# Key projection by token tiles, a norm transposed by TensorE, early FFN gradient tiles and a last store in halves, in a backward-and-forward transformer block

## The chip, the cores and the metric

The kernel runs on one core of a Trainium2 chip. The metric is device time in microseconds (us) of one execution, as the median of several runs. TensorE (PE) multiplies matrices, VectorE (DVE) and ScalarE (ACT) work on elements, GpSimd (POOL) does little here, and SyncE (SP) issues nearly all DMA transfers.

## The reference

The block has S = 2048 tokens of width D = 512, 32 heads of 16, an attention that sees 8 positions at distances 0, 2, …, 14 back, and an FFN of width F = 1792. All arrays are bf16. The kernel returns the output and the gradients of all inputs and weights.

```python
h  = x + Attn(LN(x))           # LN without scale or shift
h2 = h + FFN(LN(h))            # gelu (tanh form), b1, b2
# Attn: q,k,v = x @ wqkv; per head and position s:
#   logits[w] = q[s].k[s-2w] / 4, w = 0..7, masked where s-2w < 0
#   o[s] = sum_w softmax(logits)[w] * v[s-2w];  result o @ wo
out0, vjp = jax.vjp(f, x, wqkv, wo, w1, b1, w2, b2)
return (out0, *vjp(grad_out))
```

## The kernel before

The tokens go in four chunks of 512 (`CH`, `NC`), each of four tiles of 128 (`TPC`); D is four blocks of 128 (`DC`), F fourteen (`FT`), in the groups of `FB` (4, 4, 4 and 2). A `Plan` collects operations (`op`, `evict`, `load`, `store`, `xload`), each with its engine, what it reads and what it writes. `emit` then writes them out in the order of the table `ORDER` and with the addresses in SBUF and banks in PSUM of the table `HOMES`. So each engine does its instructions strictly in that table's order, and the costs and the `soft` arguments in the code play no part at run time. SP, too, issues its transfers in that order, and one that must wait holds up those behind it.

For each chunk, forward:

- `p1_ln` normalizes x: statistics on DVE, the power of −0.5 on POOL, the product on ACT (L398) or, for chunk 0 and what `N1V` lists, on DVE (L402). It transposes the result to `ln1T` (features on partitions): chunk 0 by PE (`to_fm_tiles`, L445: four transposes for a tile, copied out of PSUM by ACT or DVE), chunks 1 to 3 (`FM1`) by a store-free DMA transpose on SP (L277).
- `p1_qkv` and `p1_proj` project keys and queries (L674, `wk` and `wq` as weights, `ln1T` moving, 128x512) and `p1_v` the values (L699); ACT copies them to `kt`, `qt` and `tmv`. Values go to `v_d` in DRAM.
- `p1_attn`: DVE multiplies queries with shifted keys (`prf`, L517, four instructions of 128x4096 for each chunk), PE sums within heads (L525), DVE takes the maximum, PE subtracts it (L744), ACT takes exp (L747), PE transposes and sums (L752), DVE divides.
- `p1_o`: a gather on SP brings the values of 8 positions from `v_d` (`Ro`, L507); DVE makes the coefficients (`cfo`, L535) and products (`prbo`, L557, four of 128x4096); PE sums (L566), ACT copies out, PE transposes (L582).
- `p1_h`: PE multiplies with wo (L790), DVE adds x and takes statistics (L797), with a chain over ACT, `ve` on DVE (L387), POOL's power, and `nm` on DVE (L393).
- `p2_h` and `p2_out`: PE makes the first FFN matmuls (L826), ACT adds b1 (L828) and takes gelu (L831); PE makes the second (L880), DVE adds h (L882). A bias is added to h by DVE before (L809).

Backward: `p2_bwd` loads the output gradient (`gor`, four loads), transposes it by DMA to `goT`, and for each of the 14 blocks f PE multiplies goT with the transposed w2 (`w2T`, L908, four matmuls of 128x512 into a PSUM bank) and DVE multiplies this FFN input gradient by gelu's derivative (L910). `w2T` comes from DRAM by four DMA transposes of a quarter each. Then follow the rest of the FFN's backward (L922), attention's backward with three gathered products for each chunk (`p3_dots`, `p3_bands`, again L517 and L557 on DVE, L525 and L566 on PE), the input gradient (L1042), and the weight gradients (`wg_group`, L1068). These accumulate 16 matmuls of 128x512 for one 128-row block of a gradient; ACT copies it out (L283) and pairs of blocks are stored together (256 KB). The last of them are the query, value and key parts of the gradient of wqkv, in the loop over `sel`.

## Time and profile before

| what | value |
|---|---|
| median of 3 runs | 537.37 us (536.19 to 538.05) |
| profiled execution | 536.42 us, span 534.5 us, TensorE clock 0.998 |
| PE busy | 518.0 us (97%) |
| DVE busy | 475.7 us (89%) |
| ACT busy | 335.4 us (63%) |
| POOL busy | 17.0 us (3%) |
| DMA queue q1 | 131.91 MB, 96.7% of 16 engines' span |

The span runs from the first to the last instruction on the chip; the run's own time is 1.9 us longer. PE's busy time counts matmuls; loads of weights (PEld) go beside them. A group's row gives line, engine, operation, result and operands, shape and count, then the busy time in us, the mean of one in ns, and the engine's idle time ahead of it with what ended it. In timelines the first two numbers are the start and the length of a run of instructions of one kind; brackets give idle time before it. Matmuls overlap in their pipeline, so the length of one (0.379 us for 512 columns) is longer than the distance between two starts.

### The profile page before, as it was taken

To read this page: it belongs to the slowest core of one execution; us is meant where nothing else is said; L and a number is where in the kernel's file an instruction comes from. 1 tells how busy PE (TensorE), PEld (TensorE's weight loads), DVE (VectorE), ACT (ScalarE), POOL (GpSimd) and SP (SyncE) were. 2 spreads that over 40 slices of the span, in tenths; PEclk is the share of its full clock that TensorE was granted. 3 is DMA by queue.
4 is the path that set the end of the run, shared out by engine and by line. 5 is a ranking of instruction groups with operands and counts; after the bars stand their busy time and mean duration, and the time that the engine had idled before them with its cause. 6 is when DMAs were issued, how large, how long until landed. Compare 5 with 4: busy or idle time off the path is not lost.

```text
span 534.5 us, 8044 instructions
## 1 busy us (share of the span) xinstructions
PE 518.0 (97%) x2975; PEld 234.4 (44%) x3023; DVE 475.7 (89%) x607; ACT 335.4 (63%) x586; POOL 17.0 (3%) x23
## 2 busy tenths in 40 slices
...
GB/s 230 205 289 314 248 250 289 233 286 238 244 264 242 299 209 283 263 234 243 213 178 186 195 183 178 180 273 234 301 283 306 310 292 302 291 314 258 255 162 231
DMA packets 224247, 133.47 MB, mean 250 GB/s; under 512 B 180496, under 2 KB 212944, under 8 KB 220112
## 3 DMA queue, kind: packets, MB, share of 16 engines
q1 hardware_dynamic: 223824, 131.91, 96.7%
q0 software_dynamic: 384, 1.05, 0.7%
...
q14 instruction: 16, 0.13, 0.1%
...
## 4 chain that ended last, share of the span: by engine, by line
PE 70%; DVE 14%; ACT 5%; issue 4%; DMA 3%; SPq 2%; POOL 1%; DVEq 0%; ACTq 0%
PE ps L1068 23%; PE ps L922 9%; PE ps L908 8%; PE ps L1042 7%; PE ps L880 7%; PE ps L826 6%; DVE prbo L557 5%; PE ps L566 4%; PE ps L946 3%; DVE prf L517 2%; DMA Rk<-q_d 2%; ACT xb L828 1%; PE ps L525 1%; POOL rstd L390 1%; DVE st L375 1%
## 5 line engine op out<-in xcount | busy, mean ns | idle before, releaser
L908 PE MATMUL ps<-goT,w2T 128*128 128x512 bf16 x224 | 53.6, 379 | 0.1
L880 PE MATMUL ps<-w,gl 128*128 128x512 bf16 x216 | 50.5, 379 | 1.6 <-DMA w<-in_B_w_dram 1.0
L826 PE MATMUL ps<-ln2T,w 128*128 128x512 bf16 x224 | 51.1, 379 | 0.6 <-DVE st L797 0.4
L922 PE MATMUL ps<-w1T,xb 128*128 128x512 bf16 x218 | 51.0, 379 | 0.2
L604 ACT ACTIVATE gyr<-ps,rstd 128x512 bf16<-128x512 f32 x28 | 19.0, 682 | 43.5 <-PE ps L922 28.4
L1042 PE MATMUL ps<-wqkvT,gqkvT 128*128 128x512 bf16 x185 | 42.6, 379 | 0.8 <-issue 0.6
L910 DVE SCALAR_TENSOR_TENSOR xb<-xb,ps 128x512 bf16<-128x512 bf16 x56 | 36.6, 682 | 7.1 <-PE ps L908 6.9
L517 DVE TENSOR_TENSOR prb<-got,vw 128x4096 bf16<-128x4096 bf16 x16 | 36.2, 2288 | 6.1 <-PE ps L1068 2.4
L283 ACT CAST wgs<-ps 128x512 bf16<-128x512 f32 (+1 forms) x30 | 15.8, 558 | 37.8 <-PE ps L1068 37.8
L1068 PE MATMUL ps<-gw1in,ln 128*128 128x512 bf16 (+1 forms) x186 | 38.5, 352 | 0.5 <-issue 0.3
L828 ACT ACTIVATE xb<-ps,b1c 128x512 bf16<-128x512 f32 x56 | 35.5, 692 | 5.0 <-PE ps L826 4.9
L1068 PE MATMUL ps<-gor,gw2in 128*128 128x512 bf16 x164 | 38.0, 379 | 0.5 <-issue 0.3
L557 DVE TENSOR_TENSOR prbk<-Rk,cfk 128x4096 bf16<-128x4096 bf16 x16 | 35.7, 2284 | 0.5 <-DMA Rk<-q_d 0.4
L557 DVE TENSOR_TENSOR prbq<-Rq,cfq 128x4096 bf16<-128x4096 bf16 x16 | 35.8, 2284 | 0.1
L517 DVE TENSOR_TENSOR prf<-qt,kt 128x4096 bf16<-128x4096 bf16 x16 | 35.8, 2282 | 0.1
L557 DVE TENSOR_TENSOR prbo<-Ro,cfo 128x4096 bf16<-128x4096 bf16 x16 | 35.8, 2287 | 0.1
L557 DVE TENSOR_TENSOR prbv<-Rv,cfv 128x4096 bf16<-128x4096 bf16 x16 | 35.6, 2282 | 0.0
L1068 PEld LDWEIGHTS <-ln 128*128 128x128 bf16 x256 | 24.7, 98 | 24.8 <-issue 1.7
L880 PEld LDWEIGHTS <-gl 128*128 128x128 bf16 x224 | 21.6, 98 | 27.9 <-ACT mv L368 1.5
L826 PEld LDWEIGHTS <-w 128*128 128x128 bf16 x224 | 21.6, 98 | 27.8 <-issue 2.9
L908 PEld LDWEIGHTS <-w2T 128*128 128x128 bf16 x224 | 21.9, 98 | 26.6 <-issue 0.3
L922 PEld LDWEIGHTS <-xb 128*128 128x128 bf16 x224 | 21.9, 98 | 26.6 <-issue 0.3
...
## 6 DMA issues: line engine op xcount, KB each, us to landing
Ro<-v_d SPq DMA_DIRECT2D x4, 1280.0 KB, 6.2
Rq<-k_d SPq DMA_DIRECT2D x4, 1280.0 KB, 6.3
Rv<-go_d SPq DMA_DIRECT2D x4, 1280.0 KB, 7.3
Rk<-q_d SPq DMA_DIRECT2D x4, 1280.0 KB, 7.0
...
Ro<-v_d SPq DMA_DIRECT2D x4, 1024.0 KB, 8.7
Rq<-k_d SPq DMA_DIRECT2D x4, 1024.0 KB, 5.9
```

Source lines behind the costliest of these rows:

```text
L517: op("DVE", tt_us(4096), lambda g=g, pr=pr: V.tensor_tensor(out=pr(), in0=ql()[:, g, :].unsqueeze(1).to_broadcast([P, W, 512]), in1=_sub(k ...
L557: V.tensor_tensor(out=pr().rearrange("p j a (d h) -> p (j a) d h", h=H), in0=_sub(R()[:, o0, 0:1], [[1024, 4], [st, 2], [1, 512]]), in1=_s ...
L566: T.matmul(ps()[32 * j:32 * j + 32, :], lhsT=S4[:], rhs=pr()[:, j, hf, :], start=(hf == 0), stop=(hf == 1), skip_group_check=True)
L604: op("ACT", act_us(D, 1, True), lambda: A.activation(out=gyr()[:, j, :], in_=ps(), func=ACT.Copy, scale=rs[:, t:t + 1], accum_out=sg_[:, i ...
L826: T.matmul(ps(), lhsT=w1()[:, dc, f * P:(f + 1) * P], rhs=cols(ln2T[c], dc, c in FM2), start=(dc == 0), stop=(dc == DC - 1))
L828: op("ACT", act_us(512, 1), lambda f=f, ps=ps, xb=xb, f0=f0: A.activation(out=xb()[:, f - f0, :], in_=ps(), func=ACT.Identity, bias=b1c[:, ...
L880: T.matmul(ps(), lhsT=d["g"][f // 4]()[:, f % 4, j * P:(j + 1) * P], rhs=w2()[:, f, :], start=(f == 0), stop=(f == FT - 1))
L908: T.matmul(ps(), lhsT=w2T()[:, dc, f * P:(f + 1) * P], rhs=cols(goT, dc, True), start=(dc == 0), stop=(dc == DC - 1))
L910: op("DVE", 0.61, lambda f=f, ps=ps, z=z, f0=f0: V.scalar_tensor_tensor(out=z()[:, f - f0, :], in0=z()[:, f - f0, :], scalar=1.0, in1=ps() ...
L922: T.matmul(ps(), lhsT=d["d"][f // 4]()[:, f % 4, j * P:(j + 1) * P], rhs=w1T()[:, f, :], start=(f == 0), stop=(f == FT - 1))
L1042: T.matmul(ps(), lhsT=gT()[:, j, b * P:(b + 1) * P], rhs=wqkvT()[:, k0 + b, :], start=(i == 0 and b == 0), stop=(i == 2 and b == 3))
L1068: T.matmul(ps()[:, 0:N], lhsT=l, rhs=r, start=(n == 0), stop=(n == k - 1))
```

## The change

Line numbers in this section's order rows are of each program's own code: in the changed one all lines from `to_fm_pe` on are higher (L525 is L536 there, L566 L577, L674 L701, L699 L726, L744 L771, L752 L779, L826 L853, L908 L927 in the new function `gg_mm`).

1. Chunk 0's keys (`KT`): for each token tile j, 16 matmuls of 128 columns into two tiles of PSUM, so that each needs only tile j of `ln1T`. Before, 16 of 512 columns.
2. Chunk 1's norm (`FP1`) is transposed by PE, four transposes for each token tile (L456), and copied out by ACT and DVE in turn (`TFP`), in place of the DMA transpose. Two of its four norms move from ACT to DVE (`N1V`).
3. Seven of chunk 0's 14 FFN input gradient tiles (`GGE`) are made as soon as `goT` and `w2T` are there: PE's matmuls (L927), then ACT copies each to SBUF as bf16 (`gge`), and the multiplication on DVE reads that copy instead of PSUM. The loads of `gor` and the transposes of `w2T` and `goT` for this are issued early.
4. The last block of the weight gradients of wqkv is made in two halves of 256 columns, each copied out and stored by itself (`wg_halves`); the block before it is stored alone.
5. `ORDER` and `HOMES` are new.

What moves, at three places. On PE, behind the maximum of chunk 0's logits, before (`nident` subtracts it, then values of chunk 1, then the transposes of `e`):

```order
L674 MATMUL ps<-ln1T_101_16_288,wk_4_126 128x512
L744 LDWEIGHTS nident
L744 MATMUL ps<-mx_18_374,nident 128x512
L699 LDWEIGHTS ln1T_101_16_288
L699 MATMUL ps<-wv_9_192,ln1T_101_16_288 128x512
L752 LDWEIGHTS ident
L752 MATMUL ps<-e_19_399,ident 128x128
```

and now:

```order
L304 MATMUL ps<-wz_2_106 128x512
L771 LDWEIGHTS nident
L771 MATMUL ps<-mx_20_453,nident 128x512
L927 LDWEIGHTS w2T_15_309
L927 MATMUL ps<-goT_20_404,w2T_15_309 128x512
L726 LDWEIGHTS ln1T_99_18_331
L726 MATMUL ps<-wv_11_225,ln1T_99_18_331 128x512
```

The first early tile (four such matmuls) stands there; the keys of chunk 1, which stood just ahead and between the sums of the dots, now stand ahead of all of these sums. The six other early tiles follow further on in attention's forward, the last of them ahead of the first FFN matmuls.

On SP, from the loads of chunk 3 to the gather of chunk 0's values, before:

```order
L268 DMA xt_67_10_212<-in_A_x_dram 32x2x1024
L277 DMA_TRANSPOSE ln1T_101_16_288<-ln_1_79_12_244 128x16x128
L268 DMA wo_16_309<-in_A_wo_dram 128x4x512
L273 DMA v_d<-tmv_16_307 128x2x512
L273 DMA v_d<-tmv_16_296 128x2x512
L277 DMA_TRANSPOSE ln1T_123_18_342<-ln_2_109_15_305 128x16x128
L507 DMA Ro_19_380<-v_d 128x5120
L507 DMA Ro_19_380<-v_d 128x4096
```

and now:

```order
L268 DMA gor_12_277<-in_grad_out_dram 32x2x1024 x2
L277 DMA_TRANSPOSE w2T_15_309<-in_B_w_dram 128x4x448 x2
L268 DMA xt_62_11_228<-in_A_x_dram 32x2x1024
L273 DMA v_d<-tmv_18_372 128x2x512
L273 DMA v_d<-tmv_18_375 128x2x512
L277 DMA_TRANSPOSE goT_20_404<-gor_12_277 128x16x128
L277 DMA_TRANSPOSE ln1T_135_22_411<-ln_2_128_19_399 128x16x128
L518 DMA Ro_21_456<-v_d 128x5120
L518 DMA Ro_21_456<-v_d 128x4096
```

Chunk 1's DMA transpose and the load of wo are gone from there; two quarters of w2T, and goT, stand ahead of the gather `Ro`.

On DVE, the four products of chunk 1's values, with `ve` and `nm` of chunk 2's second norm between them, before:

```order
L557 TENSOR_TENSOR prbo_31_1120<-Ro_27_816,cfo_25_1062 128x4096
L557 TENSOR_TENSOR prbo_32_1123<-Ro_27_816,cfo_25_1062 128x4096
L387 TENSOR_SCALAR ve<-mv 128x4
L557 TENSOR_TENSOR prbo_35_1141<-Ro_27_816,cfo_25_1062 128x4096
L393 SCALAR_TENSOR_TENSOR nm<-mv,rstd 128x4
L557 TENSOR_TENSOR prbo_35_1159<-Ro_27_816,cfo_25_1062 128x4096
```

and now:

```order
L568 TENSOR_TENSOR prbo_30_1188<-Ro_32_933,cfo_38_1135 128x4096
L387 TENSOR_SCALAR ve<-mv 128x4
L568 TENSOR_TENSOR prbo_33_1242<-Ro_32_933,cfo_38_1135 128x4096
L568 TENSOR_TENSOR prbo_34_1244<-Ro_32_933,cfo_38_1135 128x4096
L393 SCALAR_TENSOR_TENSOR nm<-mv,rstd 128x4
L568 TENSOR_TENSOR prbo_36_1289<-Ro_32_933,cfo_38_1135 128x4096
```

`ve` stands one product earlier, and two products stand between it and `nm`.

The diff, cut to its core:

```diff
+    def to_fm_pe(src, dst, tag):
+        for j in range(TPC):
+            pt = ps_("pt" + tag)
+
+            def tr(j=j, pt=pt):
+                for dc in range(DC):
+                    T.transpose(pt.bf()[:, dc * P:(dc + 1) * P], src()[:, j, dc * P:(dc + 1) * P], ident[:])
+            op("PE", 4 * XP, tr, r=[(src, j), IDENT], w=[pt], tag="xp" + tag, lat=0.17)
+            evict(dst, lambda j=j: dst()[:, j, :], pt, lambda pt=pt: pt.bf()[:, 0:512], 512,
+                  key=("t", j), us=0.35 if TFP[j] == "DVE" else None, tag="fp%d" % j, eng=TFP[j])
...
-        if c in FM1:
+        if c in FP1:
+            to_fm_pe(ln1, ln1T, "ln1")
+        elif c in FM1:
             to_fm_dma(ln1, ln1T, "ln1")
...
+        if (tag, c) in KT:
+            pss = [ps_("psq" + tag, 2) for _ in range(2)]
+            for j in range(TPC):
+                for g2 in range(2):
+                    def mm(j=j, g2=g2):
+                        for gg in range(2):
+                            for dc in range(DC):
+                                T.matmul(pss[g2]()[:, gg * 512 + j * P:gg * 512 + (j + 1) * P], lhsT=_sub(wq_()[:, dc, 0:1], [[4, P]], 2 * g2 + gg),
+                                         rhs=st_[c]["ln1T"]()[:, dc, j * P:(j + 1) * P], start=(dc == 0), stop=(dc == DC - 1))
+                    op("PE", 8 * XP, mm, r=[wq_, (st_[c]["ln1T"], ("t", j))], w=[(pss[g2], j)], tag="kt0")
...
+    def gg_early(c):
+        gg_load(c, ())
+        st_[c]["gge"] = {}
+        for b, (f0, f1) in enumerate(FB):
+            n = min(f1, GGE) - f0
+            if n <= 0:
+                continue
+            t = sb("gge", [P, n, 512])
+            for f in range(f0, f0 + n):
+                ps = ps_("psg", 1)
+                gg_mm(c, f, ps)
+                evict(t, lambda t=t, f=f, f0=f0: t()[:, f - f0, :], ps, lambda ps=ps: ps(), 512, key=f, tag="gge")
+                st_[c]["gge"][f] = (t, f - f0)
...
+                e = d.get("gge", {}).get(f)
+                if e:
+                    t, k = e
+                    op("DVE", 0.61, lambda f=f, t=t, k=k, z=z, f0=f0: V.scalar_tensor_tensor(
+                        out=z()[:, f - f0, :], in0=z()[:, f - f0, :], scalar=1.0, in1=t()[:, k, :], op0=ALU.add, op1=ALU.mult, accum_out=gb1p[:, f, c:c + 1]),
+                       r=[(t, f)], w=[(z, f), (GB1, (f, c))], tag="gh", lock=1)
+                    continue
...
+    def wg_halves(parts, rds, dst, tag):
+
+        N, k = D // 2, len(parts)
+        st = sb("wgs" + tag, [P, D])
+        for hf in range(2):
+            ps = ps_("wg" + tag, 1)
+            for i in range(0, k, 4):
+                def mm(i=i, hf=hf, ps=ps):
+                    for n in range(i, i + 4):
+                        l, r = parts[n]()
+                        T.matmul(ps()[:, 0:N], lhsT=l, rhs=r[:, hf * N:(hf + 1) * N], start=(n == 0), stop=(n == k - 1))
+                op("PE", 2 * MM, mm, r=rds(i // 4), w=[ps], tag="wh" + tag)
+            evict(st, lambda hf=hf: st()[:, hf * N:(hf + 1) * N], ps, lambda ps=ps: ps()[:, 0:N], N, key=hf, tag="whe" + tag)
+            store(None, lambda hf=hf: dst[:, hf * N:(hf + 1) * N], st, lambda hf=hf: st()[:, hf * N:(hf + 1) * N], N / 4, skey=hf, tag="whst" + tag)
...
+    if GGE:
+        gg_early(0)
...
+GGE = 7
+KT = (("k", 0),)
...
-LSP = False
+LSH = True
 TBL = 1
-N1V = ()
+N1V = ((1, 1), (1, 3))
...
+FP1 = (1,)
+TFP = ("ACT", "DVE", "ACT", "DVE")
...
-    7, 0, 10, 8, 19, 18, 6, 5, 1, 11, 27, 4, 21, 63, 64, 65, 42, 25, 58, 59, 60, 66, 67, 69,
```

More of the change, by code (lines that the diff above doesn't have):

```diff
@@ L665, in p1_proj @@
         wq_ = wqk[sel]
+        if (tag, c) in KT:
[8 more added lines that the diff above has]
+                    op("PE", 8 * XP, mm, r=[wq_, (st_[c]["ln1T"], ("t", j))], w=[(pss[g2], j)], tag="kt0")
+            for g2 in range(2):
+                evict(dst, lambda g2=g2: dst()[:, 2 * g2:2 * g2 + 2, off:off + CH], pss[g2], lambda g2=g2: pss[g2]().rearrange("p (a n) -> p a n", a=2),
+                      1024, key=g2, tag="qkv" + tag)
+            return
         for g2 in range(2):
@@ L699, in mm @@
                             T.matmul(ps()[:, jj * 512:(jj + 1) * 512], lhsT=lt, rhs=wv()[:, dc, :], start=(dc == 0), stop=(dc == DC - 1))
-                    op("PE", len(dcs) * MM, mm, r=[wv, *([(l1, ("t", j))] if TF and c not in FM1 else lnkeys(l1, c, dcs))], w=[(ps, jj)], tag="qkvv")
+                    op("PE", len(dcs) * MM, mm, r=[wv, *([(l1, ("t", j))] if c in FP1 or TF and c not in FM1 else lnkeys(l1, c, dcs))], w=[(ps, jj)], tag="qkvv")
             if c in PM:
@@ L885, in p2_out, with gg_load, gg_mm, mm @@
             store(None, lambda ap=ap: ap, h2s, lambda j=j: slots(h2s, j), 128, tag="h2st")
+    def gg_load(c, soft):
+        d = st_[c]
+        goT = d["goT"] = sb("goT", [P, DC, CH])
+        gor = d["gor"] = sb("gor", [P, TPC, D])
+        for j, ap in enumerate(perm_rows(gof[c * CH:(c + 1) * CH, :])):
+            load(gor, lambda j=j: slots(gor, j), lambda ap=ap: ap, 128, key=j, tag="gor", soft=soft)
+        to_fm_dma(gor, goT, "go")
+    def gg_mm(c, f, ps):
+        goT = st_[c]["goT"]
+        def mm():
+            for dc in range(DC):
+                T.matmul(ps(), lhsT=w2T()[:, dc, f * P:(f + 1) * P], rhs=cols(goT, dc, True), start=(dc == 0), stop=(dc == DC - 1))
+        r = F // 4
+        op("PE", 4 * MM, mm, r=[(w2T, k) for k in sorted({f * P // r, (f * P + P - 1) // r})] + [goT], w=[ps], tag="gg")
+    def gg_early(c):
[11 more added lines that the diff above has]
+                st_[c]["gge"][f] = (t, f - f0)
     def p2_bwd(c):
         d = st_[c]
-        goT = sb("goT", [P, DC, CH])
-        gor = d["gor"] = sb("gor", [P, TPC, D])
-        for j, ap in enumerate(perm_rows(gof[c * CH:(c + 1) * CH, :])):
-            load(gor, lambda j=j: slots(gor, j), lambda ap=ap: ap, 128, key=j, tag="gor", soft=[(d["g"][1], None)])
-        to_fm_dma(gor, goT, "go")
+        if "goT" not in d:
+            gg_load(c, [(d["g"][1], None)])
+        goT, gor = d["goT"], d["gor"]
         if c < LN2R:
@@ L903, in p2_bwd @@
             for f in range(f0, f1):
+                e = d.get("gge", {}).get(f)
[5 more added lines that the diff above has]
+                    continue
                 ps = ps_("psg", 1)
-                def mm(f=f, ps=ps):
-                    for dc in range(DC):
-                        T.matmul(ps(), lhsT=w2T()[:, dc, f * P:(f + 1) * P], rhs=cols(goT, dc, True), start=(dc == 0), stop=(dc == DC - 1))
-                op("PE", 4 * MM, mm, r=[(w2T, f // 2 if W2PE else None), goT], w=[ps], tag="gg")
+                gg_mm(c, f, ps)
                 op("DVE", 0.61, lambda f=f, ps=ps, z=z, f0=f0: V.scalar_tensor_tensor(
@@ L1127, in wg_ffn @@
                                                              G_()[:, t // 4, t % 4, :] if t < 4 * KEEP else gs3[sel][t // 4]()[:, t % 4, :]) for t in range(NT)]
-                last = LSP and sel == 1 and dc > 1
+                last = LSH and sel == 1 and dc > 1
+                if last and dc == 3:
+                    PAIR.clear()
+                    wg_halves(parts, lambda c, sel=sel, G_=G_: [lp[c], (G_, c) if c < KEEP else gs3[sel][c]], out_2[dc * P:(dc + 1) * P, sel * D:(sel + 1) * D], "q")
+                    continue
                 d0 = dc - dc % 2 if last else dc - 1
@@ L1181 @@
         r = F // 4
-        xload(w2T, lambda i=i: w2T()[:, :, i * r:(i + 1) * r], lambda i=i: B_w2[i * r:(i + 1) * r, :], 448, key=i, tag="w2T", soft=[(attn, 1)])
+        xload(w2T, lambda i=i: w2T()[:, :, i * r:(i + 1) * r], lambda i=i: B_w2[i * r:(i + 1) * r, :], 448, key=i, tag="w2T", soft=() if GGE else [(attn, 1)])
     for i in range(0 if W1PE else 4):
         xload(w1T, lambda i=i: w1T()[:, :, i * P:(i + 1) * P], lambda i=i: B_w1[i * P:(i + 1) * P, :], 448, key=i, tag="w1T", soft=[(attn, 2)])
+    if GGE:
+        gg_early(0)
     for c in range(NC):
```

238 rows, old and new, of tables (HOMES, ORDER) are left out of this document.

## The prediction

> **What bounds the kernel now.** I read the page's first rows, then the busy time by stretches, then the timelines of VectorE (DVE) and TensorE (PE) where a stretch shows idle time, and last the chain of waits at the end. The page's head:
>
> ```profile
> span 534.5 us, 8044 instructions
> PE 518.0 (97%) x2975; PEld 234.4 (44%) x3023; DVE 475.7 (89%) x607; ACT 335.4 (63%) x586; POOL 17.0 (3%) x23
> ```
>
> PE is the bound on average. By stretch (its ends and length, then busy time of PE, PEld, DVE, ACT, POOL with instruction counts, PE clock, DMA share, GB/s):
>
> ```profile
> 20.00:30.00 10.00, 7.47 (x56) 2.96 (x55) 9.76 (x12) 6.83 (x11) 0.14 (x1) 1.00 1.18 237
> ...
> 80.00:100.00 20.00, 18.74 (x114) 8.26 (x117) 19.70 (x20) 19.81 (x31) 0.00 (x0) 1.00 1.05 281
> 100.00:130.00 30.00, 29.06 (x178) 12.94 (x178) 28.54 (x41) 28.04 (x48) 4.33 (x2) 1.00 0.93 242
> 130.00:250.00 120.00, 119.34 (x561) 53.84 (x572) 116.38 (x216) 107.63 (x147) 1.11 (x1) 1.00 1.03 258
> 250.00:350.00 100.00, 99.31 (x502) 44.92 (x510) 63.71 (x101) 32.52 (x70) 0.00 (x0) 1.00 1.00 191
> ...
> 450.00:508.00 58.00, 57.47 (x395) 24.79 (x400) 57.73 (x39) 27.41 (x61) 0.00 (x0) 1.00 0.98 279
> ```
>
> From 20 to 100 us DVE is full (9.76 of 10, 19.70 of 20) while PE idles 2.53 us in one slice and 1.26 in another: attention forward is bound by DVE. From 130 to 350 PE is full, and DVE idles 36 us of the last 100. From 450 to 508 DVE is full again, PE nearly so. Work that PE does early, in DVE's stage, is therefore saved later, in its own, if later work finds DVE and ScalarE (ACT) in time.
>
> **The early stage, and what the tiles save.** For PE's speed I take starts:
>
> ```profile
> 9.51 3.40 PE L674 MATMUL ps<-ln1T,wk 128*128 128x512 bf16 x15 [0.43 <-ACT ln1T L283]
> 12.96 2.75 PE L674 MATMUL ps<-ln1T,wq 128*128 128x512 bf16 x12
> ...
> ```
> ```profile
> 31.00 0.61 PE L752 MATMUL ps<-e,ident 128*128 128x128 bf16 x8 [0.25 <-ACT e L747]
> ...
> ```
>
> The program has 16 key matmuls between 9.51 and 12.96 (one record is missing): 3.45/16 = 0.2156 us for 512 columns. Eight of 128 columns in 0.61, the last 0.22 long: 0.39/7 = 0.056. I compare the two programs at one place where DVE and PE meet, the last product of chunk 1's values (prbo, L557):
>
> ```profile
> 100.80 0.17 DVE L387 TENSOR_SCALAR ve<-mv 128x4 f32<-128x4 f32 x1
> 100.87 2.29 DVE L557 TENSOR_TENSOR prbo<-Ro,cfo 128x4096 bf16<-128x4096 bf16 x1
> 104.06 0.17 DVE L393 SCALAR_TENSOR_TENSOR nm<-mv,rstd 128x4 f32<-128x4 f32 x1 [0.90 <-POOL rstd L390]
> 104.14 2.29 DVE L557 TENSOR_TENSOR prbo<-Ro,cfo 128x4096 bf16<-128x4096 bf16 x1
> ...
> 107.14 1.22 DVE L809 TENSOR_TENSOR h<-h,b2bc 128x2048 bf16<-128x2048 bf16 x1
> ```
> ```profile
> 106.51 1.04 PE L566 MATMUL ps<-prbo,S 128*32 128x512 bf16 x16
> ...
> 112.16 1.89 PE L790 MATMUL ps<-wo,oT 128*128 128x512 bf16 x8
> 114.40 7.07 PE L826 MATMUL ps<-ln2T,w 128*128 128x512 bf16 x32 [0.35 <-DVE st L797]
> ```
>
> *PE's work.* Ahead of these sums (those that start at 106.51) stand 359 matmuls of 512 columns and 72 of 128 before, 367 and 144 now: 28 for the seven early tiles (6.04 us), 16 fewer in chunk 0's keys against 64 small ones (+0.1), 16 transposes for chunk 1 (0.9), 4 others later. That is 8 × 0.2156 + 72 × 0.056 = 5.7 us more done. The whole program gets 32 matmuls of 512 fewer, 80 of 128 and 32 of 256 more (0.108, half of 512): −6.9 + 4.5 + 3.5 = +1.0. So 4.7 us less is left after the sums.
>
> *DVE's work.* Ahead of that last product DVE gets two norms and two copies for chunk 1, and one addition of a bias that stood just behind it (L809, 1.22). The groups that price this and what follows (last the busy time and the mean ns of one):
>
> ```profile
> L910 DVE SCALAR_TENSOR_TENSOR xb<-xb,ps 128x512 bf16<-128x512 bf16 x56 | 36.6, 682 | 7.1 <-PE ps L908 6.9
> ...
> L283 ACT CAST wgs<-ps 128x512 bf16<-128x512 f32 x26 | 14.5, 585 | 28.9 <-PE ps L1068 28.9
> ...
> L398 ACT ACTIVATE ln<-xt,rstd 128x512 bf16<-128x512 bf16 x12 | 9.3, 814 | 0.3 <-DMA wv<-in_A_wqkv_dram 0.3
> ...
> L283 ACT CAST wgsq<-ps 128x512 bf16<-128x512 f32 x12 | 6.6, 588 | 9.0 <-PE ps L1068 8.9
> ...
> L402 DVE TENSOR_SCALAR ln<-xt,mv,rstd 128x512 bf16<-128x512 bf16 x4 | 1.6, 412 | 0.1
> ...
> L283 ACT CAST wgs<-ps 128x256 bf16<-128x256 f32 x4 | 1.5, 384 | 8.9 <-PE ps L1068 8.9
> ...
> L287 DVE COPY ln1T<-ps 128x512 bf16<-128x512 bf16 x1 | 0.4, 424 | 0.1
> ```
> 2 × 0.41 + 2 × 0.42 + 1.22 = 2.9 us. But the new order puts two products, not one, between ve and nm, and GpSimd's power between them then has 4.5 us where 3.2 were needed: the 0.90 wait goes. DVE comes to its last product 2.0 later. PE: 2.0 later with 4.7 less to do, **−2.7 us**.
>
> *Behind it.* From 106.51 to 114.40 PE needs 7.89 us for 32 matmuls of 512 columns of work and less (6.95 us by the same pitches); 0.94 goes in waits for ACT and DVE between sums, transposes, projection and FFN. Now ff2 matmuls stand between these steps (six of them after the second transposes). I take most of that as gone, **−0.8** (bounds 0 and −0.94).
>
> The seven gradient tiles themselves: DVE's multiplication (L910, 0.68 us from PSUM) then reads SBUF. No row has this instruction with all operands there; the nearest, L402 with one of 512 columns in SBUF, takes 0.41, so 7 × 0.27 = 1.9 us less is one end, a tenth more (0.5 us) the other that I allow. I take nothing, since DVE's idle time in 250–350 lies behind it either way.
>
> *ACT* gets seven casts of 128x512 from PSUM (0.585 us by the 26 alike), two copies, and loses two norms (0.81): 4.1 + 1.1 − 1.6 = +3.6 us, all before 70 us, where it has time (6.83 busy of 10 in the slice shown). It is full from 80 on (19.81 of 20): the FFN of chunk 0 starts some 3 us later, since PE does the tiles first, so ACT's full stretch starts later too. In the old run ACT waited in that chunk for PE; in the new order the 14 evictions come closer together, so I take its end as 1 us later, which PE's matmuls for chunk 2, themselves later, don't see. If they do: up to +3.
>
> **Chunk 0's keys and the queue.** Keys by token tiles need only the first tile's transposes: PE fills part of the 0.43 wait. DVE's statistics still come before the first product, so I count nothing (bounds −0.4, +0.5). Here the row and a rule part. The Trainium skill (TensorE: Matmul & The Clock Gate, Back-to-back issue gap) says that pairs of weight load and 128-column matmul sustain about 81 ns each. By that the 80 small ones would cost 2.0 us more than I count and the sum below would be −3.0; the eight starts above are also such pairs, at 56 ns, and decide for this kernel.
>
> On SyncE's queue (SP) one transpose of 512 KB goes (chunk 1's), and ahead of chunk 0's gather Ro now stand two of w2T and one of goT, and the loads of gor, while wo and w1 wait behind it:
>
> ```profile
> 20.41 1.04 SPq L268 DMA_DIRECT2D wo<-in_A_wo_dram  x1
> 22.10 0.92 SPq L273 DMA_DIRECT2D v_d<-tmv  x2
> 24.23 3.10 SPq L277 DMA_TRANSPOSE ln1T<-ln  x1
> 27.70 0.84 SPq L507 DMA_DIRECT2D Ro<-v_d  x2
> ...
> ```
> ```profile
> Ro<-v_d SPq DMA_DIRECT2D x4, 1280.0 KB, 6.2
> ...
> Ro<-v_d SPq DMA_DIRECT2D x4, 1024.0 KB, 8.7
> ```
> ```profile
> v_d<-tmv SPq DMA_DIRECT2D x2, 256.0 KB, 5.0
> ```
> ```profile
> out_dram<-wgsq SPq DMA_DIRECT2D x6, 256.0 KB, 3.1
> ...
> out_dram<-gx SPq DMA_DIRECT2D x8, 128.0 KB, 2.4
> ...
> w2T<-in_B_w_dram SPq DMA_TRANSPOSE x4, 5.7
> ...
> goT<-gor SPq DMA_TRANSPOSE x4, 4.4
> ```
> Ro was issued at 27.70 and landed by these at 33.9 and, its second part (a little later), at about 36.8. DVE takes it up here:
>
> ```profile
> 35.70 4.50 DVE L557 TENSOR_TENSOR prbo<-Ro,cfo 128x4096 bf16<-128x4096 bf16 x2
> ```
> With 1.7 us more on DVE it is wanted at about 37.4, the second part at 41.9. One transpose more than before holds SP for some 3 us in that place, wo's 1.0 goes: Ro 2 us later, 36 and 39, is still in time. I cost it at nothing, with 1.5 us and 3 us of slack. PE's first early tile waits for goT; behind that wait stand chunk 1's values and the transposed sums of chunk 0's softmax, for which DVE waits. goT's transpose stands right behind the stores of v (22.10): issued by 23 and landed in 4.4 or, behind others, 6 us, 29 at the latest by this estimate. The tile comes after the sums of the first dots, at about 30: nothing, 2 us if goT is late.
>
> **The backward end.** The last stretch is a chain of DVE, then matmuls from 508.9 to 529.6, 20.7 us that both programs have there, then the last store:
>
> ```profile
> 506.88 1.86 PE ps L566 x32
> ...
> 520.07 9.51 PE ps L1068 x44
> ```
> PE idles 0.53 of 58 us in 450–508, DVE 0.27. DVE's share there is the same work, begun earlier by what PE gains before, since its idle time ends with PE's sums. So the gain is passed on, and I add **−0.6** for waits that may close (bounds −1.9, +2). The last weight gradient in halves: 384 ns for the last eviction instead of 588 (−0.2), and a last store of 64 KB after 256 KB. 128 KB took 2.4 against 3.1, so 64 KB should take 2.4 or somewhat less: −0.7 to −1.0. Together **−0.9** (bounds −0.3, −1.3).
>
> **Sum.** −2.7 − 0.8 − 0.6 − 0.9 = −5.0. The profiled execution took 536.42 us (span 534.5 and 1.9 around it); it becomes 531.4. It lies 0.95 below the median of the three runs, 537.37, so on their scale 532.4.
>
> **Rivals.**
> 1. *The gather comes late (slower).* If what the queue holds ran one after another, from about 17 on (an estimate: where chunk 3's loads are issued): two of w2T 11.4, the stores of v 5.0, goT 4.4, chunk 2's ln1T about as much, Ro 6.2, so Ro at 48.4, 11.0 behind the 37.4. DVE's next work needs Ro, so all of it goes on the path: −5.0 + 11.0 = +6.0, 543.4. It turns to slower than a measurement's uncertainty when Ro is over 6.6 us late. For it: DMA is over full (1.18) in 20–30. Against: Ro, issued 3.5 us behind a transpose, still landed in 6.2. Chance 0.11.
> 2. *ACT or DVE takes over between 80 and 250 (no change).* ACT has 2.2 us idle in 80–130, DVE 3.6 in 130–250. If ACT's full stretch moves by the 3 us of the later FFN start and PE waits for its gelus, −2.7 and −0.8 go and only the end's −0.9 to −1.5 stays: 536.2. For it: those shares; against: PE hardly waited for ACT there. Chance 0.13.
> 3. *The tiles aren't early.* If w2T or goT land behind 36, PE stalls at its first tile; half the gain goes: 534.9. Counted with the forecast's side, chance 0.12.
> 4. *More.* DVE's first product starts earlier, since part of chunk 2's statistics stands behind it now, by as much as DVE got to do, so that the 4.7 us count in full, and the end's waits close: −4.7 − 0.9 − 1.9 − 1.3 = −8.8, 528.6. Chance 0.12.
>
> **How the numbers follow.** The forecast has 0.52. What a measurement of this kernel tells from no change is about 0.3%, 1.6 us. Faster by more: 0.52 + 0.12 + 0.12 = 0.76; within: 0.13; slower: 0.11. The range goes from rival 4's 528.5 over the forecast and rivals 3 and 2 (536.2, and if +2 at the end comes on top, 538.0); it leaves out the slower one and a little at the lower end, less than 2 in 10.
>
> **What would show it.** Right: PE busy over 9 of 10 in most slices from 30 to 100; the nm wait of 0.90 gone; last prbo of chunk 1 at about 106; the first FFN matmul of chunk 2 near 115; sums of the last products about 4 us earlier than 506.88; the last store landing in about 2.3. Wrong: DVE idle before chunk 0's prbo with Ro as releaser; PE idle for goT; PE waiting for ACT between 120 and 180; the last prbk still ending near 507.

## The result, and the profile after

The changed kernel takes 534.77 us (median of 8 runs, 534.45 to 536.25) against 537.71 us (8 runs, 536.19 to 539.82) beside it: ratio 0.995, 95% interval 0.9934 to 0.9965. That is 2.9 us faster; 5.0 were forecast. The two profiled executions lie closer together: 536.42 and 534.75 us, spans 534.5 and 532.9. Runs of the kernel before differ in their granted clock: of 63 taken beside the experiments, the 35 with a mean of 0.992 to 0.996 have a median of 538.2 us and the other 28, with 0.997 to 1.000, one of 537.1, while all eight runs of the changed kernel have 0.999 or 1.000.

Busy time by stretches, first three rows of the kernel before that the prediction didn't show, then the changed kernel (columns as in the prediction).

```profile
0.00:130.00 130.00, 121.85 (x756) 55.39 (x766) 121.69 (x156) 107.40 (x183) 11.52 (x14) 1.00 0.92 256
...
350.00:450.00 100.00, 98.67 (x665) 46.03 (x674) 99.36 (x63) 44.37 (x94) 0.00 (x0) 1.00 1.05 287
...
508.00:534.50 26.50, 21.35 (x110) 9.44 (x103) 16.80 (x38) 16.06 (x36) 4.35 (x8) 0.96 0.71 198
```
```profile
0.00:130.00 130.00, 124.47 (x843) 60.05 (x854) 121.73 (x155) 109.54 (x187) 11.53 (x14) 1.00 0.92 262
130.00:250.00 120.00, 118.83 (x552) 53.29 (x559) 117.25 (x221) 109.37 (x148) 1.38 (x1) 1.00 1.02 246
250.00:350.00 100.00, 98.63 (x509) 44.10 (x519) 66.33 (x100) 34.08 (x77) 0.00 (x0) 1.00 0.94 194
350.00:450.00 100.00, 98.50 (x657) 46.52 (x662) 98.66 (x65) 45.08 (x92) 0.00 (x0) 1.00 1.09 287
450.00:508.00 58.00, 56.32 (x391) 24.32 (x399) 55.99 (x37) 25.93 (x60) 0.00 (x0) 1.00 1.03 290
508.00:532.90 24.90, 21.24 (x118) 10.96 (x119) 16.65 (x38) 15.50 (x32) 4.36 (x8) 0.99 0.64 177
```

By the records PE is busy 518.0 us in both, so the spans differ by idle time. PE's idle time falls by 2.62 us up to 130 (8.15 to 5.53), rises by 0.51, 0.68, 0.17 and 1.15 in the four stretches to 508, and falls by 1.49 behind them: −2.62 + 2.51 − 1.49 = −1.60, the difference of the spans. A gain is made early, given back in the middle, and made again at the tail. The single stretches in the middle are not to be read closer than that: both traces lack matmul records (2975 for 3023 weight loads before, 3056 for 3103 now), and a missing record can count as idle time. The trace of experiment 7, which lacks none and whose program is the same up to 508, has 0.77, 0.80, 0.21 and 0.96 us of idle time in those four stretches, where the changed kernel's has 1.17, 1.37, 1.50 and 1.68. The waits that name another engine, shown below, don't have this fault.

The early gain is the forecast one. VectorE's and TensorE's timelines at the place that the prediction priced:

```profile
101.27 0.17 DVE L387 TENSOR_SCALAR ve<-mv 128x4 f32<-128x4 f32 x1 [0.31 <-ACT jks L369]
101.35 4.49 DVE L568 TENSOR_TENSOR prbo<-Ro,cfo 128x4096 bf16<-128x4096 bf16 x2
105.77 0.15 DVE L393 SCALAR_TENSOR_TENSOR nm<-mv,rstd 128x4 f32<-128x4 f32 x1
105.84 2.28 DVE L568 TENSOR_TENSOR prbo<-Ro,cfo 128x4096 bf16<-128x4096 bf16 x1
```
```profile
30.83 1.02 PE L927 MATMUL ps<-goT,w2T 128*128 128x512 bf16 x4
...
108.07 1.05 PE L577 MATMUL ps<-prbo,S 128*32 128x512 bf16 x16
...
112.11 3.62 PE L817 MATMUL ps<-wo,oT 128*128 128x512 bf16 x16
115.56 1.67 PE L853 MATMUL ps<-ln2T,w 128*128 128x512 bf16 x7
```

The nm row has lost its wait, the last product starts at 105.84 (forecast 106.1), and chunk 2's FFN at 115.56, 1.16 us later than before. PE's idle time up to there is 4.80 us instead of 7.93, a lead of 3.1. From there to the last matmul's end (529.58 before, 529.45 now) 3.0 of the 3.1 go. Two of the places:

```profile
125.95 1.05 PE L577 MATMUL ps<-prbo,S 128*32 128x512 bf16 x16 [0.73 <-DVE prbo L568]
...
255.12 7.07 PE L927 MATMUL ps<-goT,w2T 128*128 128x512 bf16 x32 [0.79 <-ACT gyr L615]
```

Between 116 and 400 TensorE waits five times for another engine: 0.73, 0.28 (at 146.7) and 0.18 (at 215.9) for VectorE, 0.79 for ScalarE, 0.24 (at 379.9) for VectorE, 2.2 in all. The traces of experiments 7 and 9 have the same five, within 0.04 us each. At the last products come 0.39 and 0.72, also for VectorE. Before, the waits from there to the tail are 0.29 and 0.17, so these 3.3 less 0.5 are the loss, to about 0.2. The last of it is the plainest. VectorE, TensorE and SyncE's queue at the end of the backward pass, in the changed kernel:

```profile
492.97 2.29 DVE L568 TENSOR_TENSOR prbv<-Rv,cfv 128x4096 bf16<-128x4096 bf16 x1
...
498.96 8.96 DVE L568 TENSOR_TENSOR prbk<-Rk,cfk 128x4096 bf16<-128x4096 bf16 x4 [1.86 <-PE ps L1127]
```
```profile
505.77 1.48 PE L577 MATMUL ps<-prbk,S 128*32 128x512 bf16 x24 [0.39 <-DVE prbk L568]
507.97 0.61 PE L577 MATMUL ps<-prbk,S 128*32 128x512 bf16 x8 [0.72 <-DVE prbk L568]
```
```profile
486.59 1.72 SPq L277 DMA_TRANSPOSE gqkvT<-gks  x1
488.36 1.19 SPq L273 DMA_DIRECT2D out_dram<-wgs  x1
489.59 0.98 SPq L518 DMA_DIRECT2D Rk<-q_d  x2
490.62 10.44 SPq L277 DMA_TRANSPOSE gqkvT<-gqs  x1
```
```profile
Rk<-q_d SPq DMA_DIRECT2D x1, 1280.0 KB, 9.2
```

and before:

```profile
490.98 1.63 SPq L507 DMA_DIRECT2D Rk<-q_d  x2
```
```profile
498.83 8.89 DVE L557 TENSOR_TENSOR prbk<-Rk,cfk 128x4096 bf16<-128x4096 bf16 x4
```
```profile
Rk<-q_d SPq DMA_DIRECT2D x1, 1280.0 KB, 7.0
```

VectorE stands idle for 1.86 us ahead of the last four products. The row names TensorE, whose matmul had long ended; what came at that moment is the Rk gather, issued at 489.59 and landed 9.2 us later, at 498.8. Before, it was issued at 490.98 and landed in 7.0. So although everything ahead is earlier, the last products start 0.1 us later than before.

How VectorE's lead goes, by the starts of its big products in the two timelines:

| product | before | after | lead |
|---|---|---|---|
| first dots of the backward pass | 306.15 | 302.97 | 3.18 |
| first prbv, chunk 1 | 427.44 | 424.51 | 2.93 |
| first prbk, chunk 2 | 478.53 | 476.08 | 2.45 |
| last prbv, chunk 3 | 493.95 | 492.97 | 0.98 |
| first prbk, chunk 3 | 498.83 | 498.96 | −0.13 |

The two programs put VectorE's small steps in different places, so not every fall of the lead is a wait. Two reductions (`jk` with its `sx`, 1.35 us together) that stood behind the last prbv now stand ahead of it and make most of the fall from 2.45 to 0.98. From the first prbk of chunk 2 to that of chunk 3 VectorE is busy 20.94 us instead of 20.16 and idle 1.94 instead of 0.14: 0.8 of the 2.6 lost there is order, 1.8 is the wait.

### The profile page after: what moved, and what is told of

The parts are those of the page before. It is cut to its first block, busy times and chain, and to the rows that moved or that the text cites. A ratio compares the mean times of both kernels' runs of the same rounds, so it can differ in the third digit from the quotient of the medians.

```text
span 532.9 us, 8240 instructions
## 1 busy us (share of the span) xinstructions
PE 518.0 (97%) x3056; PEld 239.2 (45%) x3103; DVE 476.6 (89%) x611; ACT 339.5 (64%) x594; POOL 17.3 (3%) x23
## 5 line engine op out<-in xcount | busy, mean ns | idle before, releaser
L927 PE MATMUL ps<-goT,w2T 128*128 128x512 bf16 x224 | 53.7, 379 | 1.1 <-ACT gyr L615 0.8
L853 PE MATMUL ps<-ln2T,w 128*128 128x512 bf16 x224 | 51.3, 379 | 0.5 <-DVE xb L969 0.5
L969 DVE SCALAR_TENSOR_TENSOR xb<-xb,ps 128x512 bf16<-128x512 bf16 x49 | 32.1, 681 | 2.6 <-PE ps L927 2.2
L927 PEld LDWEIGHTS <-w2T 128*128 128x128 bf16 x224 | 21.7, 98 | 28.3 <-issue 2.7
L853 PEld LDWEIGHTS <-w 128*128 128x128 bf16 x224 | 21.5, 98 | 28.1 <-issue 3.4
```

What stands on the lines that cost most here:

```text
L853: T.matmul(ps(), lhsT=w1()[:, dc, f * P:(f + 1) * P], rhs=cols(ln2T[c], dc, c in FM2), start=(dc == 0), stop=(dc == DC - 1))
L927: T.matmul(ps(), lhsT=w2T()[:, dc, f * P:(f + 1) * P], rhs=cols(goT, dc, True), start=(dc == 0), stop=(dc == DC - 1))
L969: op("DVE", 0.61, lambda f=f, ps=ps, z=z, f0=f0: V.scalar_tensor_tensor(out=z()[:, f - f0, :], in0=z()[:, f - f0, :], scalar=1.0, in1=ps() ...
```

## The experiments

All start from the changed kernel, 534.77 us; "first theory" is that of the run's own text. Ratios are to the kernel before, run beside each.

### 1. The last gather two places earlier

```diff
 SP: DMA Rv<-go_d 128x4096
+    DMA Rk<-q_d 128x5120
+    DMA Rk<-q_d 128x4096
     DMA_TRANSPOSE gqkvT<-gks
     DMA out_dram<-wgs
-    DMA Rk<-q_d 128x5120
-    DMA Rk<-q_d 128x4096
     DMA_TRANSPOSE gqkvT<-gqs
```


> Nothing is left out: the two parts of chunk 3's Rk gather are issued two places earlier in SP's program, ahead of a gks transpose and a wgs store (in the trace of the changed kernel these took SP from 486.59 to 489.55; the gather was issued at 489.59 and landed at 498.84, and VectorE stood idle for 1.86 us until 498.96, when the last four prbk products began). First theory: the lead that TensorE and VectorE bring out of the forward stages is still there at 497, and the late gather is what takes the last of it; then the last prbk products begin 1.3 to 1.9 us earlier, the last sums of the band follow, and the time falls by 1.0 to 1.8 us. Rival: TensorE's own queue sets the end whatever the last gather does, since it has weight-gradient matmuls to fill the wait; then the products begin earlier and the time changes by less than 0.4 us.

543.03 us (1.0098, 1.0067 to 1.013): 8.3 us slower. SyncE's queue, TensorE's timeline and one stretch of this kernel:

```profile
486.19 0.80 SPq L518 DMA_DIRECT2D Rk<-q_d  x2
487.86 7.47 SPq L277 DMA_TRANSPOSE gqkvT<-gks  x1
495.37 0.58 SPq L273 DMA_DIRECT2D out_dram<-wgs  x1
```
```profile
497.44 6.43 PE L1101 MATMUL ps<-wqkvT,gqkvT 128*128 128x512 bf16 x16 [4.48 <-DMA gqkvT<-gks]
```
```profile
490.00:500.00 10.00, 5.52 (x26) 1.82 (x25) 8.11 (x11) 0.60 (x1) 0.00 (x0) 0.82 1.13 324
```

Both theories fell. The transpose that now stands behind the gather holds SP for 7.47 us instead of 1.72, TensorE waits 4.48 us for it, and the granted clock drops to 0.82: the next 16 matmuls take 6.43 us. The four products started at 505.3.

### 2. Fewer matmuls in the late tiles

```diff
-            for dc in range(DC):
-                T.matmul(..., start=(dc == 0), stop=(dc == DC - 1))
+            k = 1 if c == 0 and f >= GGE else DC
+            for dc in range(k):
+                T.matmul(..., start=(dc == 0), stop=(dc == k - 1))
```


> Seven FFN input-gradient tiles of chunk 0 (those that the change leaves late, at 141 to 150 us) get one of their four matmuls, so those tiles' values are incomplete: 21 matmuls of 128x512 fewer at 215.6 ns, 4.5 us of TensorE work taken from the stage in which the early lead was being given back. First theory: TensorE's work is passed on until the last Rk gather stops it, so the time falls by 0.3 to 1.5 us and VectorE waits longer for that gather than the 1.86 us of before. Rival: VectorE, ScalarE and the gathers set the pace from 130 us on whatever TensorE has to do; then the sums of the last band move by under 0.3 us and the time by less than 0.3 us.

Each of the seven late tiles gets one of its four matmuls. 536.46 us (0.9969, 0.9953 to 0.9986): not faster; the median is 1.7 us higher, which the intervals don't clearly separate. The stretch from 140 to 160, in the changed kernel and here, and the first dots product here:

```profile
140.00:160.00 20.00, 19.53 (x89) 8.67 (x90) 19.80 (x50) 19.94 (x21) 0.00 (x0) 1.00 0.98 222
```
```profile
140.00:160.00 20.00, 16.08 (x69) 6.57 (x70) 19.82 (x50) 19.94 (x21) 0.00 (x0) 1.00 1.00 242
```
```profile
303.05 2.28 DVE L528 TENSOR_TENSOR prb<-got,vw 128x4096 bf16<-128x4096 bf16 x1
```

The work taken out comes back as 3.4 us of idle TensorE at once; DVE and ACT are full as they were (19.82 and 19.94 of 20), and the dots start at 303.05 instead of 302.97. In this stage ScalarE and VectorE set the pace, as the rival has it; which of the two isn't separated. The profiled execution (539.21) was this kernel's slowest of ten and lost 2.5 us waiting for the Rk gather of chunk 0 (products at 413.3 instead of 410.7); whether the median really rises is not settled by it.

### 3. Both edits

```diff
 (the lines of 2, and in SP's program)
+    DMA Rk<-q_d x2
     DMA_TRANSPOSE gqkvT<-gks
     DMA out_dram<-wgs
-    DMA Rk<-q_d x2
```

> Both edits: 21 matmuls fewer at 141 to 150 us (their tiles' values are incomplete) and the last Rk gather two places earlier on SP. First theory: with the gather out of the way more of the TensorE work taken out is passed to the end, so the two gains add up to more than their sum apart: the time falls by 2.0 to 4.0 us. Rival (VectorE, ScalarE and gathers set the pace): the time equals that of the kernel with the earlier gather alone, within 0.4 us.

542.96 us (1.0094, 1.0067 to 1.0121), that of experiment 1. The new wait hides what was asked; experiment 12 asks it again.

### 4. Late tiles done twice

```diff
-            for dc in range(DC):
+            for dc in [*range(DC)] * (2 if c == 0 and f >= GGE else 1):
```


> The seven late FFN input-gradient tiles of chunk 0 (141 to 150 us) have their four matmuls done twice, with the same values: 28 matmuls of 128x512 more at 215.6 ns, 6.0 us of TensorE work added where the seven early tiles of the change used to be. First theory: TensorE is full there (118.8 of the 120 us from 130 to 250) and what it loses is carried to the end: the time rises by 4.5 to 6.0 us. Rival: TensorE has slack against VectorE and the gathers, so the time rises by 2 us at most; on that theory moving seven tiles out of this stage could never have brought more than that.

542.22 us (1.0076, 1.0048 to 1.0104), 7.4 us slower; its profiled execution took 539.66. The same stretch and product:

```profile
140.00:160.00 20.00, 19.90 (x92) 9.11 (x93) 18.82 (x45) 18.99 (x21) 0.00 (x0) 1.00 0.98 227
```
```profile
308.32 2.28 DVE L528 TENSOR_TENSOR prb<-got,vw 128x4096 bf16<-128x4096 bf16 x1
```

Now TensorE is the full engine (19.90), and 5.35 of the 6.0 us reach the dots. With experiment 2: TensorE is less than a microsecond short of setting the pace there. The early tiles take it below that edge, and every microsecond beyond is worth nothing.

### 5. The early tiles undone

```diff
-                evict(t, lambda t=t, f=f, f0=f0: t()[:, f - f0, :], ps, lambda ps=ps: ps(), 512, key=f, tag="gge")
-                st_[c]["gge"][f] = (t, f - f0)
+                op("ACT", 0.4, lambda: None, r=[ps], w=[(t, f)], tag="gge")
+                st_[c]["gge"][f] = (t, ps)
...
-                        ... in1=t()[:, k, :], op0=ALU.add, ...
+                        ... in1=k(), op0=ALU.add, ...
```
with the seven gg operations moved to a few places ahead of their products.

> Nothing is left out: the seven FFN input-gradient tiles of chunk 0 are made late again, one bank of PSUM each, a few places ahead of the product that reads them, and their seven evictions fall away; all else of the change stays. 28 matmuls of 215.6 ns (6.0 us) go back to 125 to 150 us. First theory, after the run in which the late tiles were done twice (6.0 us more TensorE work there: the first dots product of the backward pass began at 308.3 instead of 303.0): the early tiles are what carries the change's gain, and without them the dots begin 3 to 5 us later and the time rises by 3 to 7 us. Rival: VectorE sets the pace from 130 to 300 us, since 4.5 us less TensorE work there left the first dots product at 303.1; then the tiles bring little, the dots begin within 1 us of 303.0 and the time rises by 1 us at most.

543.82 us (1.0125, 1.0102 to 1.0149), 9.1 us slower. A stretch and the first dots product:

```profile
60.00:80.00 20.00, 16.34 (x128) 7.24 (x131) 19.73 (x16) 14.11 (x26) 1.01 (x1) 1.00 0.92 288
```
```profile
311.05 2.28 DVE L528 TENSOR_TENSOR prb<-got,vw 128x4096 bf16<-128x4096 bf16 x1
```

TensorE idles 3.7 us from 60 to 80 (0.8 in the changed kernel), and the dots come 8.1 later: the tiles carry the gain, and more than the 6.0 us of their matmuls.

### 6. Chunk 1's norm turned by DMA

```diff
             def tr(j=j, pt=pt):
-                for dc in range(DC):
-                    T.transpose(pt.bf()[:, dc * P:(dc + 1) * P], src()[:, j, dc * P:(dc + 1) * P], ident[:])
+                if j == TPC - 1:
+                    SY.dma_start_transpose(out=_sub(dst()[:, 0, 0:1], [[P, 16], [1, P]]), in_=src().rearrange("p j d -> p (j d)"))
...
-            evict(dst, lambda j=j: dst()[:, j, :], pt, lambda pt=pt: pt.bf()[:, 0:512], 512, ...)
```


> Nothing is left out: chunk 1's normalized input is turned by one transposing DMA of 512 KB again (issued by SP where the last of the four TensorE turns stood, between two w2T transposes) instead of by 16 TensorE transposes and four evictions. First theory: the turned input comes later by the time of that DMA in a queue of transposes (the w2T parts took 5.1 us from issue to landing) less 16 transposes and an eviction (1.5 us), so TensorE waits 2 to 4 us between 18 and 30 us, the last product of chunk 1's outputs begins 1.5 to 3.5 us after 105.8, and the time rises by 1 to 3 us. Rival: TensorE fills the wait with the keys of chunk 0, the values and early tiles, and the time stays within 0.5 us.

540.16 us (1.0041, 1.0029 to 1.0053), 5.4 us slower, more than expected. VectorE, TensorE and the stretch around it:

```profile
23.85 2.29 DVE L527 TENSOR_TENSOR prf<-qt,kt 128x4096 bf16<-128x4096 bf16 x1 [4.34 <-DMA ln1T<-ln]
```
```profile
23.80 5.75 PE L700 MATMUL ps<-ln1T,wk 128*128 128x512 bf16 x16 [4.52 <-DMA ln1T<-ln]
```
```profile
20.00:30.00 10.00, 6.20 (x19) 2.50 (x20) 6.15 (x4) 4.49 (x7) 0.60 (x1) 0.66 1.05 215
```

TensorE and VectorE wait 4.5 and 4.3 us for the DMA, and the clock falls to 0.66 on top. TensorE needs what the DMA writes. VectorE's product belongs to chunk 0 and doesn't: by `HOMES` its result (`prf`) lies in the 64-byte units 3092 to 3219, over chunk 1's `ln` (3171 to 3234), and the DMA must have read that before VectorE may write there. In the changed kernel TensorE has read it by then. So the 5.4 us are the price of the DMA together with one tile's home; the DMA with that tile elsewhere wasn't run, and what turning by TensorE is worth by itself isn't shown. VectorE's delay of 4.4 at the first dots of the backward pass (307.4) is still 4.6 at the last prbk (503.5).

### 7. The last store whole

```diff
-                    for n in range(i, i + 4):
+                    for n in range(i, i + 4) if hf == 0 else ():
-                        T.matmul(ps()[:, 0:N], lhsT=l, rhs=r[:, hf * N:(hf + 1) * N], ...)
+                        T.matmul(ps()[:, 0:D], lhsT=l, rhs=r, ...)
```
and one eviction of 512 columns and one store of 128 KB.

> Nothing is left out: the last weight-gradient group is made in one piece of 512 columns, with one eviction and one store of 128 KB, in place of two halves of 256 columns with a store of 64 KB each. First theory: the eviction takes 0.2 us longer (588 ns against 373) and the last store 0.5 to 1.1 us longer (128 KB landed in 3.8 us, 64 KB in 2.7), so the time rises by 0.7 to 1.3 us. Rival: another transfer ends last (the gx stores on the other queue) and the time stays within 0.3 us.

535.49 us (0.9959, 0.9945 to 0.9973); 0.7 more, which these intervals don't separate from nothing. The last eviction and the last store, of the changed kernel, then here, and then the last store of the kernel before:

```profile
529.49 0.37 ACT L283 CAST wgsq<-ps 128x256 bf16<-128x256 f32 x1 [1.37 <-PE ps L1147]
```
```profile
out_dram<-wgsq SPq DMA_DIRECT2D x1, 64.0 KB, 1.9
```
```profile
529.25 0.59 ACT L1149 CAST wgsq<-ps 128x512 bf16<-128x512 f32 x1 [2.00 <-PE ps L1147]
```
```profile
out_dram<-wgsq SPq DMA_DIRECT2D x1, 128.0 KB, 1.7
```
```profile
out_dram<-wgsq SPq DMA_DIRECT2D x1, 256.0 KB, 3.0
```

A last store of 128 KB lands as fast as one of 64, one of 256 KB some 1.2 us later; the halves save an eviction's 0.2 us. From the last matmul's end to the span's end it is 4.9 us before, 3.6 here (from 529.2), 3.45 with halves: most of the tail's gain is that the last group is no longer stored together with the one ahead of it.

### 8. The gather one place earlier

```diff
     DMA_TRANSPOSE gqkvT<-gks
+    DMA Rk<-q_d 128x5120
+    DMA Rk<-q_d 128x4096
     DMA out_dram<-wgs
-    DMA Rk<-q_d 128x5120
-    DMA Rk<-q_d 128x4096
     DMA_TRANSPOSE gqkvT<-gqs
```


> Nothing is left out: the two parts of chunk 3's Rk gather are issued ahead of the wgs store in front of them (1.19 us on SP) but stay behind the gks transpose, which in the run with the gather ahead of it was held on SP for 7.5 us and left TensorE idle for 4.8. First theory: the gather lands 1.0 to 2.0 us earlier than 498.84, VectorE's wait of 1.86 us shrinks by as much, and the time falls by 0.5 to 1.5 us. Rival: the DMA engines are full there (busy share 0.92 to 1.07 of them from 480 to 500), so the gather lands when it did, or TensorE's queue sets the end, and the time stays within 0.4 us.

543.25 us (1.0092, 1.0079 to 1.0105), 8.5 us slower; both theories fell again. The store's landing, then ScalarE, TensorE and VectorE:

```profile
out_dram<-wgs SPq DMA_DIRECT2D x1, 256.0 KB, 9.4
```
```profile
502.44 0.69 ACT L615 ACTIVATE gyr<-ps,rstd 128x512 bf16<-128x512 f32 x1 [8.16 <-DMA out_dram<-wgs]
```
```profile
503.94 2.75 PE L577 MATMUL ps<-prbv,S 128*32 128x512 bf16 x24 [5.89 <-ACT gyr L615]
```
```profile
506.74 4.50 DVE L568 TENSOR_TENSOR prbk<-Rk,cfk 128x4096 bf16<-128x4096 bf16 x2 [6.74 <-PE ps L577]
```

Behind the gather the store lands 9.4 us after its issue (2.6 in experiment 1, where it went later). A gyr tile of chunk 2 has its home on the store's source, so ScalarE waits 8.2 us to write it, TensorE 5.9 for ScalarE, VectorE 6.7 for TensorE.

### 9. The same, with another home for that tile

```diff
 (the two lines of 8, and)
+HOMES[711] = 320
```


> Nothing is left out: the last Rk gather ahead of the wgs store, as in the last run, and one buffer moved: the gyr tile of chunk 2 that was written over that store's source (ScalarE waited 8.2 us for the store, which landed behind the gather) gets a home that no transfer reads. First theory: with that wait gone the gather lands 1 to 2 us earlier than 498.84 in the changed kernel, VectorE's wait of 1.86 us shrinks and the time is 0.5 to 1.6 us under that of the changed kernel; then the gather was what took the last of the lead. Rival: TensorE and the DMA engines set the end, and the time is within 0.5 us of the changed kernel's.

534.41 us (12 runs; 0.9946, 0.993 to 0.9963). VectorE in its profile:

```profile
498.00 8.89 DVE L568 TENSOR_TENSOR prbk<-Rk,cfk 128x4096 bf16<-128x4096 bf16 x4
```

One changed home takes 8.8 us off, which proves the cause in 8. VectorE's wait for the last gather is gone, and TensorE has none over 0.2 us from 480 to 512; its idle time from 450 to 508 is 0.63 instead of 1.68. Its five waits between 116 and 400 are all still there. In this execution VectorE was 1.0 us later than in the changed kernel at 477.1 (0.5 of it since its first product, at 16.8) and 1.0 earlier at the last prbk, so 2.0 are recovered in that stage; the span is 0.6 shorter. The median is 0.4 us under the changed kernel's, short of the 0.5 expected, and the intervals don't tell the two apart: a gain isn't shown.

### 10. The gather two places earlier, with that home

```diff
 (the lines of 1, and)
+HOMES[711] = 320
```


> Nothing is left out: the gather ahead of the gks transpose too, with the gyr tile in its new home. First theory: a transposing DMA behind a gather holds SP until the gather has landed (7.5 to 10.4 us in the rows so far, against 1.7 to 3.0 elsewhere), so gks comes 5 to 6 us later, TensorE idles 4 to 5 us for it with its clock lowered behind that, and the time is 4 to 8 us over the changed kernel's although VectorE gets its gather early. Rival: the waiting ScalarE alone made the two slow runs slow; then this one is as fast as the run with the gather behind the gks transpose, within 1 us.

542.08 us (1.0083, 1.0067 to 1.0099), 7.3 us slower, as the first theory has it. SyncE and TensorE:

```profile
488.74 7.87 SPq L277 DMA_TRANSPOSE gqkvT<-gks  x1
```
```profile
498.83 6.35 PE L1101 MATMUL ps<-wqkvT,gqkvT 128*128 128x512 bf16 x16 [4.98 <-DMA gqkvT<-gks]
```

With the home out of the way the held transpose costs the same by itself. The two causes are separate, and either is enough.

### 11. Chunk 0's keys whole

```diff
-                        for gg in range(2):
+                        for gg in range(2 if j == (3, 0)[g2] else 0):
                             for dc in range(DC):
-                                T.matmul(pss[g2]()[:, gg * 512 + j * P:gg * 512 + (j + 1) * P], ..., rhs=...[:, dc, j * P:(j + 1) * P], ...)
+                                T.matmul(pss[g2]()[:, gg * 512:(gg + 1) * 512], ..., rhs=...[:, dc, :], ...)
```
(each half where the last tile that it needs is there)

> Nothing is left out: chunk 0's keys made with matmuls of 512 columns once all four tiles of the turned input are there, in place of matmuls of 128 columns by tiles. 64 pairs of 56 ns (3.6 us) become 16 of 215.6 ns (3.4 us), but none of them can begin before the last tile's eviction, some 5 us after the first. First theory: the first products of the forward pass come 0.5 to 2.5 us later than 16.3 us, VectorE passes that on (a delay of 4.4 us at 24 us was still 4.5 us at 503 us in the run with the norm turned by DMA) and the time rises by 0.5 to 2.5 us. Rival: the products wait for the k tile's own path, which is ready as early, and the time stays within 0.4 us.

534.89 us (0.9952, 0.9937 to 0.9968): no difference, the rival. The first product starts at 16.8, as it does in other executions with the keys by tiles (16.1 to 17.0).

### 12. Fewer matmuls with the gather out of the way

```diff
 (the lines of 9, and)
-            for dc in range(DC):
+            k = 1 if c == 0 and f >= GGE else DC
+            for dc in range(k):
```

> The kernel with the last Rk gather ahead of the wgs store and the gyr tile in its new home (534.41 us; no wait of VectorE or TensorE over 0.3 us from 480 to 510), and 21 matmuls of the late tiles left out at 141 to 150 us (4.5 us; those tiles' values are incomplete). First theory (VectorE sets the pace from 130 to 300): the 4.5 us come back as idle time of TensorE before 160, the first dots product stays within 0.7 us of 303.0 to 303.7, and the time within 1.0 us of 534.41. Rival (the earlier run without these matmuls gained nothing only because gathers behind it landed late): with the last gather out of the way the time falls by 1.5 to 4 us.

535.53 us (0.9953, 0.9937 to 0.9969), 1.1 over experiment 9; first dots at 303.18, TensorE busy 16.19 of 20 from 140 to 160. VectorE at chunk 0's Rk gather:

```profile
413.60 2.29 DVE L568 TENSOR_TENSOR prbk<-Rk,cfk 128x4096 bf16<-128x4096 bf16 x1 [2.65 <-DMA Rk<-q_d]
```

No gain, a tenth beyond the first theory's margin. The wait at the last gather is gone, but chunk 0's gather comes late, as it did in the execution of experiment 2 (2.48 us), so the medians of 2 and 12 may contain that wait. What they show of the late tiles rests on what lies ahead of it: TensorE's work taken out comes back as idle time before 160, and the dots are no earlier.

## Why the prediction was right in sign and too large

*The handoff, −2.7 and −0.8: right.* The sums start at 108.07, 1.56 later than before with the 4.7 less to do that the prediction counted: −3.1. From there to the FFN it is 7.49 us instead of 7.89, though eight more transposes (0.45 by the same pitch) stand in it: −0.85. So the prediction's own count gives 4.0 for the forecast 3.5, and PE's idle time gives 3.1. This is one execution: in nine runs of experiments 1 to 4, 7 to 10 and 12, whose programs are the same up to 115, PE's idle time up to there is 4.4 to 6.5 (4.80 here), and of the kernel before there is one trace. Experiment 5 shows what carries the lead: without the early tiles the kernel loses 9.1. Experiment 6's 5.4 contains a wait that one tile's home makes, so the share of the turn by TensorE stays open. Such prices don't add up to the change's 2.9, since the order was laid around all its parts; the kernel before had an order of its own.

*Costed at nothing: mostly right.* The multiplication from SBUF took 685 ns, from PSUM 681. The first early tile ran at 30.83 without a wait (about 30 forecast). Ro was issued at 28.34, and VectorE took it up at 37.24 without a wait for it; its second part landed at about 39, as forecast. The keys by tiles were worth nothing (experiment 11); 48 of their matmuls took 2.84 us with the last one's 0.22, 56 ns each with a weight load in every pair, so the 81 ns of the Trainium skill (TensorE: Matmul & The Clock Gate, Back-to-back issue gap) don't hold for these either.

*The lead unseen by the full engines, rival 2: this step failed in part.* The prediction put at nothing that PE might wait for ACT or VectorE behind 80. From 120 to 160 ScalarE is busy 39.84 of 40 us and VectorE 39.41, and experiments 2, 4 and 12 show that TensorE has less than a microsecond to gain there before these two hold it. TensorE's five waits between 116 and 400 take 2.2 us (0.3 from there to 400 before); four of them name VectorE and one, 0.79, ScalarE. The sign named for this, PE waiting for ACT between 120 and 180, was not there; PE waiting for VectorE was. VectorE itself still had a lead of 3.2 at the first dots, so rival 2's full loss didn't come about.

*The backward end, −0.6, "the gain is passed on": this step failed.* Of VectorE's 3.2 at 303, 2.4 are left at 476 and nothing at 499. The argument counted work on VectorE and TensorE and took the gathers as being there. The new order has the wgs store ahead of the last gather, and the gather took 9.2 us instead of 7.0; experiment 9 shows that the 1.86 us wait goes when the gather goes one place up, and 8 and 10 why it can't simply do so. At TensorE the late products cost 1.1 us of waits where 0.6 were to be gained, which is within the bound of +2 that stood beside the term. The sign named for this, the last prbk still ending near 507, was there: 507.9. But with that wait gone the median fell by 0.4 us only, inside the noise, so the gather explains little of what is missing by the medians.

*The tail, −0.9: too small.* −1.5 in the profiled executions. The last eviction gives the forecast 0.2. The last store landed in 1.9 us where 3.0 were needed before, 1.1 for a forecast of 0.7 to 1.0; 0.2 are not accounted for. Experiment 7 shows that the halves' smaller store has no part in it: 128 KB landed in 1.7, so the gain is from the last two groups no longer being stored together.

*The sum.* In the profiled executions, by TensorE's idle time: 3.1 early, 3.0 given back, 1.5 at the tail, 1.6 in all. The medians differ by 2.9, since the profiled execution of before lies 1.3 below the median of its 8 runs and that of the changed kernel on it. Which stage makes the runs of before spread over 3.6 us and those of the changed kernel over 1.8 stays open.
